# A refitted build-time timing model and a new order of work in a one-core attention and feed-forward kernel

## The chip, the core and the metric

The kernel runs on one core of a Trainium2 chip. A core has a matrix engine (TensorE, shown as PE, with its weight loads as PEld), a vector engine (VectorE, DVE), an activation engine (ScalarE, ACT), a general engine (GpSimd, POOL) and a queue engine that only issues transfers (SyncE, SP). Each engine runs its own instruction list in order, and the lists meet through semaphores. The metric is the device time of one execution in microseconds (us).

## The reference

The input `x` has 2048 rows of 640 values. After a layer norm it goes through two branches, which are added to the input:

```python
xn  = layernorm(x)
q   = (xn @ wq) -> 32 heads of width 20;  k = xn @ wk;  v = xn @ wv   # one k and one v for all heads
p   = softmax(q k^T * 20 ** -0.5)          # 32 heads x 2048 x 2048
A   = (p v, heads side by side) @ wo
B   = silu(xn @ w1) @ w2                   # 640 -> 1728 -> 640
out = x + A + B
```

The scores are the large object: 32 x 2048 x 2048 values pass through an exponential.

## The kernel before

**Tiling of the attention.** The queries are cut into four chunks of 512, the keys into 16 tiles of 128. One *block* is the score tile of one head, one query chunk and one key tile: 128 keys by 512 queries, which is one PSUM bank. There are 32 x 4 x 16 = 2048 blocks. Four heads make a group, and consecutive blocks go round the four heads. The head width is 20, padded to 32, so a score matmul uses 32 of the 128 rows of TensorE and four blocks of four different heads run side by side (L1182, called S below). A fifth block of the same run has to wait for the row strip of the first.

**Exponentials.** A block takes one of two ways. On ScalarE one `Exp` activation reads one to four adjacent banks and writes bf16 (L1217). On VectorE one instruction turns the scores into 16-bit integers whose bits, read as bf16, approximate the exponential (L1234); three such blocks make a set, and for a set two shifted copies are made: one on VectorE or GpSimd, the other always on GpSimd (L1262 and L1268). A ScalarE block needs one matmul with the values `v`, a VectorE block three. Four of these matmuls, one per head, make one step called P (L1079), which adds into bank 7, kept for it. The other seven banks serve the score blocks and the third kind of matmul.

**Other work.** Projections, the feed-forward branch and the output projection run as steps called J (L541), four matmuls of 32 columns side by side, 512 or 320 wide. The feed-forward branch also needs 54 `Tanh` activations (L1456).

**What sets the order.** The instruction lists are made at build time by a planner. It keeps a clock for each engine, and gives every operation a modelled duration and a time at which its result is seen by others (`LAT`). For ScalarE, VectorE and GpSimd it takes the next ready operation by priority. TensorE follows from block 70 on a written string, `ORDER`, one letter for each action (`follow`, L860). `P` and `J` are the steps named above. Any other letter is a *visit*: it issues the S matmuls of the next 1 to 4 blocks, and `VISITS` says how many blocks and how many of them go to VectorE. Upper case puts the first shifted copy of a set on VectorE, lower case on GpSimd. A visit waits until the planner's model has enough banks free (`s_banks`, L706) and until the exponentials' buffer of 26 slots has room (`room`, L931); if it has none, P steps are put in ahead of it. In `do_S` (L1143) the planner chooses the banks, orders the S matmuls by the modelled time at which each bank comes free, and forms one `Exp` for each run of adjacent banks. S matmuls planned for the same moment share one semaphore increment, that of the last of them (`seal`, L1139).

The planner's times are not in the program. The program has only the order on each engine, the choice of banks, the cut into `Exp` instructions, the side of each shifted copy, and the waits that follow.

Of the kernel before, what the change touches and what calls it, by code (L numbers as in the profile page):

```python
# [22 lines left out]
S = 2048  # L23
# [42 lines left out]
SWITCH = 0.106  # L66
FIRST = 0.01
T_PE = 0.2155
S_AGAIN = 0.09
REL = {"act": 0.07, "dve": 0.04}  # L70
LATE = 0.2
T_S = 0.2085
S_GAP = 0.0035
S_LEAD = 0.9
PV_PRESS = 12
DVE_TH = 0.6
# [9 lines left out]
ORDER = (
    "KmkmmkPhKFPgkPPPKMmgMPPCKPgPfPPgMPKhPCKPPmGPHJkBJJPBJbPPJJGmJJJJmkmPKKKPPMkkPMkmBJPkKMPJPJhkPJKkmJPH"
    "KPMKPFkPPMkkPJPMKhPPbJJGkJcMKJkPgHHBhPPghKmPemJPPJJJJPGhKJJPMJBJmgJmgPJJJJJPPPPBPBPBPJGMPJbMGPPbPPGJ"
    "PKkhPPPJPFJPKmPPkGMPPJJJBJJbPPfPPkKmPPJJPJKkMPJPJPfPJJJJJJJMAJPJJJJmkKMkJJPJBKPPPPBPPMGKJJJJPJMGmkPJ"
    "PPPJPPPfJPPJPPJMMgKJJJJJMgKJPJJJKmbPJCPPaPJJkmPJmMkkJJPgGPJJPJJhkmJJJPJJmaJJJJJPgmPBMPPPBPPMGMPPGMJP"  # L90
    "JBJJJPJJMGkkMJJPJPgmJJPgmPJPJkkmPfPPPBPPMaPJPPJPBJJJPBPmgPJPJbJJPJbJPJPmgJJJJJGmJJBPPFMKKPPbMPPPaJJG"
    "mJJPJPbJJJJMkKPJJJGMPJJMKKPPfbPMkkPPmgMAPPJPJPJgMJJPBPMKKJJJJPJPmGPJPJbJJJPgMJJJJKMKPEfPPPbPPFPPBJPP"
    "PJgmPPJJPGMJJaPJJBJJJJJJEPPPPfPPPMgPFPPJJGMJBJJMGJPPJbPJJPJJJPPPPKGJPPJJJPJJFPPJGPPMBPPmGPPPKGmPPPFP"
    "PBPJPJPJBMGJJPJPPgmJJgMJJPGMJJJJGmPfPgmePJJJBPJJgmPJJMGJJPJmMAkPPPPPHkPJJPMgMJJJPmKHkJJJJPJmKGJPJJJk"
    "HPcPJmHgJJJJJKBbmPPGmPPKhPJJJJJBbPPPJJPJPbJgMJPbPJJJJJBJJJJJgmbPPPPPgmmPPbPJPbJJJJbgmPPPPPGMmPPPBPPJ"
    "JJBJJbbJJJJJbGMMkKPPkmgPPPJPJPPbMJJPJPGbJJJJJbPPmKkmPPPgMPJJMGJPJJPEHPPPPBJJJJBJPJkKmJJJJgMJJJJJmkKJ"
    "JJJhKFfbhHPPgMPAPPPJJPgMJJJPaMPbPPPPfPJPgJPMKMKJPJPPJPPJGmJJmgJJJgmJJJJJMgJJPBPJAPfPPPPMMGPmmGgJJJJP"
    "JJBJmGPJJPJPbJJPGmmGJJJPPJBPPJJbJPmgPPFPPbPPJKgJJJJbmbPPBJPJGMPJJMgJJJmGJJPMgJPJgMJPPmGPBPJJmGJPJJGm"
    "JJbPPPkmGPPgMJPJJJJgKMJJJPJJPMKgMJJJJKMKPPJgmJJPJbPJmgmhKPPKkMPEPPPPfPPmgPBJJmgJJJbPfPPgmPJJJJPMkkBJ"
    "JJJJJJJEJPJJJKhJPJJPBPPmkKkPPPPPMCGPPPmKKPJPJmGPPPPJGMPPJJJgmPJPPJbJJJJbJJbPJJbPJhKPmgPJJmgPFPPMGMmG"  # L100
    "PPJJGJJPJPPPJPgMkJJPJPkKPJJGmmJPJPJBJBJJPJJBPPEPPPPfPPbPPbPPfPPbPJJJJJbGMPPPJJPJgmPBJJJJJMAmJJPEPJPJ"
    "PJkmJJePJJJJJPbBPPPPPbmPhKPJJGmJJPJMGKPPPPPbBPPJJPJGMmJJPJJPhGmJJJJJJFJJPEJJPJJJPgMmGPPPPMgJPJPBJPJb"
    "JPBPPPmKkMPkHPJJJBJbPJJJbPJJJGMPJJJhKJmGPJPGmPPFPPBJJJJJgkMkmPPPJJPfJJJGmgmAPPbPPJPJbmJPPbJGMPJgmJPJ"
    "BPPJMgJJJmGJPgmJPJJJamJPPPJcGJPJJMKkJPJJgMPPbmPPkgPPJPBMJJPGJJJFPJJJJgmJJJbJPJgMPbJJJJPmABJJPJPeJJPP"
    "bbMPPmgPPPBmPBmgPPPhHPJGJPPJKMgJJJJJBJJmgJPJJkkmJJJJKmkJPJBmPPKHMAPPJPPJPJJBJPHkJPkMkJPJJJmkgJJJJPbJ"
    "PJKmKJPJJHBPPPMaPPPPcKPPbPPmkkPPKmkMJJPJBJJgMPHkJPmGPPJPJPfJPPPPJJHkmkPJJPJJJmKKkJJJJJPmkkJPPJJfBPBP"
    "FPPgmPPGMJJJMGJJJbJPJPmgPJJmGJPgMJJPBJPPbJJBPJJGmBJPPbPPEJJJPJMgJPPJJJPkBPJJJJJJkmGJJPPMbPJPJmgMgJPP"
    "bPPMbPPKmkPPEPJPJJJJMGPJJBJJJJmgPBJJJBJJJJmgJmgPPfPPBPPgmKPPHkPJPPJJhJPJJGhPJJJPJePPPPMgPPFPPBJJJbJJ"
    "bJJPJPcJJPePJJJJJKmKHKPPPPPPPgkMHPPPPmBJJPJKkMJPJJPmbKJPJJJMAPJJJJJGkmmJJJJJPPgmGmPPPPPkhMJJJJJemKPP"
    "PPPKHmJJJbmPJJPggMJPJPPPgMJJkmPJmAPJJJHJJPmGBPPPPPPbPPJJJPJmGJJJJGmJPJmGJJBPJJmgJJPJbJPJmGPfPgmPPPBP"  # L110
    "PHGPJJJJJJGKMJPPJJJkmBJJJJBJJJJJBFPPAPPPfPPPPFPPGmJJJJMgJJJHkPPPJaJJJPJPPKMkJPJPJJJJJCkPambPPPPmkMKP"
    "kkMfPbPPPPJPJgmJPbJPJPJBBJPPJbPBJPPJgMPJJBPJJJMgJJJJmGPAMPJPPJJJJPbJJJBJPJBPJJBmgJJJJkmkJJJPMkaMGMPP"
    "PPMaPPPPFPPGmPPPPFPBPJPJbJJbPPJGMJPJJPmgJbPPJJPJJMAJJPJJBPJJgmPPBMPPBPPPMAPPGmPPJJJPJJEJJJJJJgMPJBJJ"
    "JJbJJJfPbPBPPmMgePmGPJPJJJEPPJPJPJBJPJJJmGPPJPJBJPJPPJbPPJBJbPPJgmPPFbPBFPPbPMbGMbPPmGMgBPPPGPPPaPMG"
    "PPPPPmPgmPPeMgMPbMPePmGPPPPPBPPMaBJJJJJJBJPJBPEPPAP"
)
Z_COST = 0.2
U_PRIO = 1.022
# [40 lines left out]

class Op:  # L160
    __slots__ = ("eng", "dur", "fn", "deps", "prio", "seq", "end", "avail", "idx", "inc", "inc_no", "sem",
                 "on_sched", "name", "dma", "mode", "start", "mm", "work", "then", "lock", "rep", "tile", "kt", "w", "x", "na", "at")

    def __init__(self, eng, dur, fn, deps, prio=0.0, name="", on_sched=None, mode=None):
        self.eng = eng
# [28 lines left out]
class Sched:  # L194
    def __init__(self, nc, stack):
        self.nc = nc
        self.stack = stack
        self.engs = ("pe", "act", "dve", "pool", "sp")
        self.order = {e: [] for e in self.engs}
        self.t = {e: 0.0 for e in self.engs}  # L200
        self.pend = {e: [] for e in self.engs}
        self.lastw = {}
        self.readers = defaultdict(list)
        self.seq = 0
        self.nsem = 0
# [48 lines left out]
    def ready(self, op, extra=0.0):  # L254
        r = op.at
        for d in op.deps:
            if d.avail is None:
                return INF
            if d.eng == op.eng and not d.dma:
                if op.eng == "pe" or op.eng == "sp":  # L260
                    a = d.end
                else:
                    a = d.avail - OWN[op.eng]
            else:
                a = d.avail
# [12 lines left out]

    def commit(self, op, start):
        e = op.eng  # L280
        op.start = start
        op.end = start + op.dur
        if op.dma:
            if op.name in ("oTd", "xTd", "uTd"):
                self.dma_t = op.end
            self.dma_t = max(getattr(self, "dma_t", 0.0), op.end) + op.mode / (270e3 if op.end < 13.5 else RATE)
            op.avail = op.end + T_LAND.get(op.name, 1.6) if op.name in ("oTd", "xTd", "uTd") else max(op.end + 2.0, self.dma_t + 1.6)
        else:
            op.avail = op.end + LAT[e]
# [160 lines left out]
class Builder:  # L450
# [692 lines left out]
    def do_S(self, n, now, nd=None):  # L1143
# [919 lines left out]
```

## Time and profile before

| | |
|---|---|
| median of three runs | 680.37 us (lowest 678.98) |
| the profiled execution, its own time | 680.39 us |
| its span, first to last instruction | 678.6 us |
| PE busy | 670.4 us (99%) |
| ACT busy | 662.1 us (98%) |
| DVE busy | 615.3 us (91%) |
| POOL busy | 566.2 us (83%) |
| granted TensorE clock | 0.997 |

The profiled execution took 1.8 us more than its span. "Busy" is the time in which at least one instruction of the engine is in flight. Instructions of one engine overlap, so a busy share close to 100% doesn't say by itself that the engine could take no more: what counts is the distance from one instruction to the next.

### The profile page before, as it was taken

What the parts mean: (1) busy time and instruction counts of PE and PEld (TensorE: products, weight loads), DVE (VectorE), ACT (ScalarE), POOL (GpSimd) and SP (SyncE); (2) the same over time, 40 slices, a digit from 0 to 9 for tenths busy, and PEclk for the clock granted to TensorE, in tenths of its full rate; (3) what the DMA queues carried; (4) which work ended last, traced back from release to release, by engine and by line L of the source; (5) the groups of instructions that cost most, each with busy time, mean ns of one, the idle gap of its engine ahead of it and who ended that gap; (6) DMA issues with size and microseconds to landing.
All of it is one profiled execution on the core that took longest, in us unless ns stands there. A gap on an engine that the chain in (4) does not pass through costs nothing.

```text
span 678.6 us, 22121 instructions
## 1 busy us (share of the span) xinstructions
PE 670.4 (99%) x9663; PEld 239.9 (35%) x9663; DVE 615.3 (91%) x1093; ACT 662.1 (98%) x852; POOL 566.2 (83%) x466
## 2 busy tenths in 40 slices
PE   9999999999999999999999999999999999999998
PEld 4433233333333333333333333333333333333324
DVE  8799989998999999999899899899989998998996
ACT  6899999999999999999999999999999999999996
POOL 6588898888878988886989987988898999878873
PEclk9899999999999999999999999999999999999999
DMA  7358300001003000101102000011012100000003
GB/s 207 79 196 269 80 18 15 7 15 15 18 17 57 10 10 17 36 15 32 29 19 60 10 18 21 27 17 33 14 29 47 31 2 20 10 19 19 20 17 64
DMA packets 51895, 27.81 MB, mean 41 GB/s; under 512 B 37750, under 2 KB 51158, under 8 KB 51798
## 3 DMA queue, kind: packets, MB, share of 16 engines
q1 hardware_dynamic: 51510, 26.07, 15.2%
q8 instruction: 75, 1.23, 0.8%
q10 hardware_dynamic: 288, 0.33, 0.1%
q14 instruction: 22, 0.18, 0.1%
HBM read 11.44 MB, written 2.62 MB: 21 GB/s over the span
## 4 chain that ended last, share of the span: by engine, by line
PE 50%; ACT 49%; issue 0%; DVE 0%; ACTq 0%
ACT sbt L1217 47%; PE psall L1079 17%; PE psall L1182 16%; PE psall L541 15%; ACT sbt L1456 2%; PE psall L999 1%; PE psall L1954 1%; PE psall L1446 0%; PE psall L1358 0%; PE psall L1935 0%; PE psall L1378 0%; ACT sbt L1803 0%; ACT sbt L1559 0%; PE psall L1498 0%; PE psall L1332 0%
## 5 line engine op out<-in xcount | busy, mean ns | idle before, releaser
L1217 ACT ACTIVATE sbt<-psall 128x1024 bf16<-128x1024 f32 (+2 forms) x773 | 632.1, 1001 | 3.6 <-PE psall L1182 3.2
L1268 POOL TENSOR_TENSOR sbt<-sbt 128x768 int32<-128x768 int32 (+2 forms) x376 | 525.0, 1424 | 84.2 <-DVE sbt L1262 78.4
L1234 DVE TENSOR_SCALAR sbt<-psall 128x512 int16<-128x512 f32 x708 | 461.2, 684 | 45.8 <-PE psall L1182 39.4
L1079 PE MATMUL psall<-sbt 128*32 128x512 bf16 x3464 | 284.2, 383 | 0.0
L1182 PE MATMUL psall<-sbt 32*128 32x512 bf16 x2048 | 258.1, 385 | 2.6 <-ACT sbt L1217 1.8
L541 PE MATMUL psall<-sbt 128*32 128x320 bf16 (+1 forms) x3863 | 239.0, 331 | 0.0
L1182 PEld LDWEIGHTS psall<-sbt 32*128 32x128 bf16 x2048 | 70.1, 91 | 226.5 <-ACT sbt L1217 124.8
L541 PEld LDWEIGHTS psall<-sbt 128*32 128x32 bf16 x3863 | 89.4, 95 | 88.5 <-issue 44.9
L1079 PEld LDWEIGHTS psall<-sbt 128*32 128x32 bf16 x3464 | 75.3, 95 | 103.2 <-issue 69.3
L1262 DVE TENSOR_SCALAR sbt<-sbt 128x1536 int16<-128x1536 int16 (+2 forms) x112 | 60.3, 552 | 0.3
L1464 DVE SCALAR_TENSOR_TENSOR sbt<-sbt,psall 128x512 bf16<-128x512 bf16 (+1 forms) x56 | 37.9, 678 | 0.2 <-ACT sbt L1456 0.2
L1456 ACT ACTIVATE sbt<-psall 128x512 bf16<-128x512 f32 x54 | 36.0, 666 | 0.0
L1300 POOL TENSOR_TENSOR sbt<-sbt 128x320 bf16<-128x320 bf16 x31 | 22.6, 729 | 5.6 <-DVE sbt L1262 4.8
L1312 DVE CAST sbt<-psall 128x512 bf16<-128x512 f32 x31 | 21.1, 682 | 0.6 <-PE psall L1079 0.4
L999 PE MATMUL psall<-sbt 128*128 128x512 bf16 (+6 forms) x56 | 15.5, 416 | 1.9 <-DVE sbt L1717 1.2
L1562 DVE SCALAR_TENSOR_TENSOR sbt<-psall,sbt 128x320 bf16<-128x320 f32 x28 | 13.3, 486 | 1.7 <-PE psall L541 1.4
L1413 DVE TENSOR_SCALAR sbt<-psall 128x512 bf16<-128x512 f32 (+1 forms) x19 | 13.0, 683 | 0.8 <-PE psall L541 0.4
L1783 DVE BATCH_NORM_STATS2 sbt<-sbt 128x6 f32<-128x320 bf16 x26 | 11.3, 465 | 2.4 <-DMA sbt<-in_A_x_dram 2.4
L1809 POOL TENSOR_SCALAR sbt<-sbt 128x640 bf16<-128x640 bf16 x8 | 7.0, 874 | 6.4 <-DVE sbt L1813 3.4
L999 PEld LDWEIGHTS psall<-sbt 128*128 128x128 bf16 x56 | 5.4, 108 | 8.9 <-issue 3.8
L1295 DVE RECIPROCAL sbt<-sbt 128x16 f32<-128x16 bf16 x31 | 7.5, 244 | 0.0
L1954 PE MATMUL psall<-sbt 128*128 128x256 bf16 x40 | 6.8, 310 | 0.6 <-ACT sbt L1217 0.6
(87 smaller groups left out, 81.0 us busy)
## 6 DMA issues: line engine op xcount, KB each, us to landing
sbt<-in_A_x_dram SPq DMA_DIRECT2D x31, 160.0 KB, 3.5
out_dram<-sbt SPq DMA_DIRECT2D x15, 160.0 KB, 1.8
sbt<-in_B_w_dram SPq DMA_DIRECT2D x5, 432.0 KB, 5.1
sbt<-sbt SPq DMA_DIRECT2D x105, 20.0 KB
sbt<-in_B_w_dram SPq DMA_DIRECT2D x13, 160.0 KB, 2.8
sbt<-sbt SPq DMA_DIRECT2D x1, 1024.0 KB, 7.3
sbt<-sbt SPq DMA_TRANSPOSE x56, 2.4
sbt<-in_A_wo_dram SPq DMA_DIRECT2D x5, 160.0 KB, 2.9
```

The source lines that it names most:

```text
L541: ins = pe.matmul(self.bk(b, 0, n, j, j + SLOT), w[:, j:j + SLOT], x, start=start, stop=stop, tile_position=(0, j), skip_group_check=True)
L999: return pe.matmul(self.bk(b, 0, n), self.zero[:, 0:P], self.zero[:, 0:n], start=True, stop=True)
L1079: ins = pe.matmul(self.bk(UBANK, 0, QW, r, r + SLOT), self.v[:, it.w, it.kt, :], it.x(), start=f, stop=False, tile_position=(0, r), skip_g ...
L1182: return pe.matmul(self.bk(bank[i]), self.kT[r:r + SLOT, 1 if i in dv else 0, kt * P:(kt + 1) * P], self.qT[r:r + SLOT, g % 8, (g // 8) % ...
L1217: return a.activation(self.E[:, (b0 + lo) * QW:(b0 + lo + m) * QW], self.ps[:, b * BANK:(b + m) * BANK], AF.Exp, scale=ACT_SCALE)
L1234: return v.tensor_scalar(self.Z[:, zs, zp * QW:(zp + 1) * QW], self.bk(bb), 0.0, ZMAX, ALU.max, ALU.min)
L1262: sc.new("dve", td, lambda v, k=k: v.tensor_scalar(self.Y[:, zs, k, 0:w], self.Z[:, zs, 0:w], float(PH[k + 1][0]), None, ALU.add), zk, yk, ...
L1268: sc.new("pool", tp, lambda v, k=k, cb=cb: v.tensor_tensor(self.Y[:, zs, k, 0:w].bitcast(I32), self.Z[:, zs, 0:w].bitcast(I32), cb, ALU.ad ...
L1300: op = sc.new(eng, 0.75 if eng == "pool" else t_dve_ps(16 * DH), lambda v: v.tensor_tensor(dst, ut[:, :, :, 0:DH], rb, ALU.mult), [key, (" ...
L1312: ev = sc.new("dve", t_dve_ps(QW), lambda v: v.tensor_copy(self.U[:, up, :], self.bk(UBANK)), [("UB",)], [("U", up)], prio=U_PRIO, name=f" ...
L1456: sc.new("act", t_act(QW), lambda a: a.activation(t, src, AF.Tanh, scale=0.5), [("B", b)], [("tb", tp)], prio=X_PRIO, name=f"th{c}_{fk}")
L1464: sc.new("dve", t_dve_ps(QW), lambda v, r0=r0, r1=r1, ht=ht: v.scalar_tensor_tensor(out=ht[r0:r1, :], in0=t[r0:r1, :], scalar=1.0, in1=src ...
```

## The change

The model's constants and rules are changed, and the string is another one. No operation is added to the kernel's mathematics.

In the model: a visit's S matmul is charged 0.092 instead of 0.106 us for entering its mode, the step after a visit up to 0.1315 us, an activation's completion can run behind its issue (each activation completes no sooner than its duration plus 0.0125 us after the one before it), a bank is counted free from that completion, some pairs of engines get their own latency, and S matmuls planned within 0.037 us of each other share an increment, with their increments 0.037 us apart.

In the string the actions are, counted from the two versions:

| | before | after |
|---|---|---|
| P letters / J letters | 860 / 936 | 862 / 934 |
| visits | 1055 | 701 |
| visits of 1 / 2 / 3 / 4 blocks | 502 / 252 / 232 / 69 | 75 / 112 / 377 / 137 |
| blocks in all, on VectorE, on ScalarE | 1978, 694, 1284 | 1978, 698, 1280 |
| visits with 0 / 1 / 2 / 3 / 4 ScalarE blocks | 321 / 237 / 444 / 53 / 0 | 62 / 69 / 500 / 69 / 1 |
| unbroken runs of visits (no P or J between) | 531 | 527 |
| further rounds of four blocks in these runs | 91 | 90 |
| sets whose first copy is on GpSimd / VectorE | 116 / 115 | 109 / 123 |

The first 70 blocks are issued before the string begins, in both. Two new forms of visit are there, `i` (four blocks, all on ScalarE, used once) and `l` (two blocks, both on VectorE, used 12 times). The diff, with the two strings cut to their first and last lines:

```diff
-REL = {"act": 0.07, "dve": 0.04}
+REL = {"act": 0.075, "dve": 0.045}
...
+S_IN = 0.092
+P_IN = 0.1315
+INC = 0.037
+ACT_MORE = 0.0125
+PAIR = {("act", "dve"): 0.17, ("dve", "pool"): 0.163}
...
-VISITS = {"a": (3, 0), "b": (3, 1), "c": (3, 2), "e": (4, 1), "f": (4, 2), "g": (2, 0), "h": (2, 1), "k": (1, 0), "m": (1, 1), "d": (4, 3)}
+VISITS = {"a": (3, 0), "b": (3, 1), "c": (3, 2), "e": (4, 1), "f": (4, 2), "g": (2, 0), "h": (2, 1), "k": (1, 0), "m": (1, 1), "d": (4, 3), "i": (4, 0), "l": (2, 2)}
 ORDER = (
-    "KmkmmkPhKFPgkPPPKMmgMPPCKPgPfPPgMPKhPCKPPmGPHJkBJJPBJbPPJJGmJJJJmkmPKKKPPMkkPMkmBJPkKMPJPJhkPJKkmJPH"
...
-    "PPPPPmPgmPPeMgMPbMPePmGPPPPPBPPMaBJJJJJJBJPJBPEPPAP"
+    "hkCblgbfACBPPAcPPPBPBfJJJMgcPJJhPggPPJFJPJJJbgmMPPPHPPJAPJPPPCPJPeJPFJkPGPEcPPBFPPJbPaJCJJJEBLAJBJPB"
...
+    "BJJBJJJPbPBPPJJbJBJPBPJFJPPmGBPFbPPPBePPBPPPfPPbPfAPPFPPbhPPMEKPmkPPBPPPfPPMgPPePPJJJGJPPFPGJJPIP"
 )
...
+                if self.fine and not d.dma and (d.eng, op.eng) in PAIR:
+                    a += PAIR[d.eng, op.eng] - LAT[d.eng]
...
-            op.avail = op.end + LAT[e]
+            op.cmp = op.end
+            if e == "act":
+                op.cmp = self.act_done = max(op.end, self.act_done + op.dur + ACT_MORE) if self.fine else op.end
+            op.avail = op.cmp + LAT[e]
...
-                    r = max(r, d.end + REL[d.eng])
+                    r = max(r, d.cmp + REL[d.eng])
...
+        if self.pe_mode == "S" and mode != "S" and 0 <= self.at:
+            return max(P_IN - SWITCH, P_IN - idle)
...
-        dur = T_S + SWITCH if timed else T_PE + 0.004 * (n > 3) + self.switch("S")
+        dur = T_S + S_IN if timed else T_PE + 0.004 * (n > 3) + self.switch("S")
...
-            if timed and due[i] > at + 1e-9:
+            if timed and due[i] > at:
+                if due[i] > at + INC:
+                    self.seal(group)
+                    group = []
                 at = due[i]
-                self.seal(group)
-                group = []
...
+        if timed:
+            heads = [sop[i] for i in turn if sop[i].rep is None]
+            for a, c in zip(heads, heads[1:]):
+                if c.avail < a.avail + INC:
+                    for q in sop:
+                        if q is c or q.rep is c:
+                            q.avail = a.avail + INC
```

More of the change, by code (lines that the diff above doesn't have):

```diff
@@ L84 @@
 YIELD = 0.65
-VISITS = {"a": (3, 0), "b": (3, 1), "c": (3, 2), "e": (4, 1), "f": (4, 2), "g": (2, 0), "h": (2, 1), "k": (1, 0), "m": (1, 1), "d": (4, 3)}
+VISITS = {"a": (3, 0), "b": (3, 1), "c": (3, 2), "e": (4, 1), "f": (4, 2), "g": (2, 0), "h": (2, 1), "k": (1, 0), "m": (1, 1), "d": (4, 3), "i": (4, 0), "l": (2, 2)}
 ORDER = (
-    "KmkmmkPhKFPgkPPPKMmgMPPCKPgPfPPgMPKhPCKPPmGPHJkBJJPBJbPPJJGmJJJJmkmPKKKPPMkkPMkmBJPkKMPJPJhkPJKkmJPH"
[L88 to L114, printed above, removed]
-    "PPPPPmPgmPPeMgMPbMPePmGPPPPPBPPMaBJJJJJJBJPJBPEPPAP"
@@ new lines @@
+    "hkCblgbfACBPPAcPPPBPBfJJJMgcPJJhPggPPJFJPJJJbgmMPPPHPPJAPJPPPCPJPeJPFJkPGPEcPPBFPPJbPaJCJJJEBLAJBJPB"
+    "PJJbPmgJhJPGmBPBPJJPBPPJPPPbPJPEPPBPJJJJJBblGPBPPPBPPkbPJPJPfPJJPJPGBJJJJJBfPPBPPJPPbPPPJPHkJJJPfJJJ"
+    "JJPEJJJJJJBhJJJJPhGPPPBPPFJJJJJBgPJPPJJFJJPPBHJJJJPJJePJJPJfJPPPKePPJJHPJJePJPPKfJPJPPPBJJJPJPbJJJJJ"
+    "PmgbPJPJJPGlPbPPPfPPBJJJJBJPPJJBBPPJPPJPPBJJJbPJJbPPfBPPPePJPJJBPPJJPPPMGJPPPJPbPJJbJgMPJJBPJJPJJJbJ"
+    "JPBPPGLPbPPPBPEPPPJJJbPJPGPFJJJPJBPJPbJPJbJJJPmGPHgPPPPfJPJJPbJBJPBJbPJJJPbJJJJbPJJPBJbPJJJPePPPFPPP"
@@ new lines @@
+    "BPFPPJJBJJPBJJJaPJJPJbJJJJBPePPPPfPPPPfPAPJJJbJJPbJJJJbJJJPBPJbJJJPBJJJbfPPBEPPPPFPPbPJPJaJKLJPJPJBP"
+    "BJJJJbJJJbJfPhkePPJJPJbJJbPJPMGJJJJBBPPPPPBPJJJmbJJPPbhPJJJJJPehPPJJJFPPJJbhJPJJJJePPPPPBPFPPBJPJbJP"
+    "GmJPJBPPPJJJJJbPPJJbJJJBJJJJJPHePPPPPBPMbPJPJCJJJbPPbPPPFPPMgJPJJBJJBBJJPBJPJJMgPPPgMPPkbPJPJPJPPlGJ"
+    "JPPBgJJJJJbPPFPPBPJPBJJJJePPPPPkMbJJJPbJJJJJBJJbJJJJJhkJJJJbFbfBPBPPEPPJPJbJPJJAPPfPPPPfPPJgPJPFJJJP"
+    "JbJJGMJPJJJJfGJJPJJJJbfPPBFEPJPJJKFJJPPbJPMkKJJPJJPgbPPJJJJJJPJfJJPgPPbPFPPPBPPEPJJPbPJbJJPFPBPPbPJJ"
@@ new lines @@
+    "BJJJJJBJPPBJPJbJJBJJJGmJPJBJPJPmGePJJJJbPPPJPPJPJEJPJPJJCGJPPBPJJbJPJBJPPbJJPbPFPPPPhgPPPFPPJJbJPbJb"
+    "JPPbPPFPPbJJJJbJbJJJJJJEJJPJJbJJJJbPPePPPPPhFPPPBPPBJPJJbJJJbJJPBJJBJJJbPJBJPBJPBPPJJJBPmgMPKgfPJPJJ"
+    "JJJbJPJBJJPbJJJbFJJgJPPJePJPPJbPBMPPPBPPGlPPbJPJbJJJbBPPPPPJPJPbPJPPbJPPPJBJJJJJbPBPJPPPJJJJPbbPPJJJ"
+    "JJMGBPPPPPfPPBJJCJJJPEPPPPBPPPPkGJJJPBmJJPPJmhgJJPJJCkPJJJJJeJJJJPJPBmgPPPPBPJPJbPPPJPJbJPPbPbPPFPPJ"
+    "PPJBPJJJfgPPPJJBJJJbJJJPBJJBfPJJbJJJPFGPBJJJJJfgPhKPPPeJPJJbJHkJPPPFPBPJPJbPJJBJJJBPJJBPJPBJPJBPbJJJ"
@@ new lines @@
+    "JBJPJJBPPGlPPaPPPPbbPPJPJJJMbJJJJGJJJGmmJJPJJbJJJJbPghBPPJJJJPePPPPPJPPPBbPfPBPPFPPPbPPEPPPJPJPJBPJJ"
+    "JJbPJBJJJJJBJbJJJJJbfPPBPEPPJPJPJJbJPJPJBPbJJJJBJJJBBPJBJJJJbfPPBPEPPPPFPPbPJPJJBbPJJPPfPPbPBJJJJbPJ"
+    "JJJPPJJbbPJJJJJbJJJbJfPPbFPBPPJPBJJbJPJPamPPJJJEPPJFPJJJJBJPbJJPbJJbPJPBPPPEPPJJPJPBJPJJBJJPJBJJPBJJ"
+    "JBPJbJJPbPJJPGmPfPPPBPPbPPeJJJPJBJJPbJJJPBJPBJJJJBJPJJbJPJBPfBPPePJPJBPJPPJJPePJJPJhJJEPPPPbPPPBmPPb"
+    "PJJBPJmgJcJJJJJJJeJPPJJJlGGbPPhhPJJPBJPbJPJPPJkhHPJJJPJPalJJJJJHgJPJPPBJcJPJPeJJJJJPbBPPPPPFPPBJPPGm"
@@ new lines @@
+    "JJJJPbKMkPPPJJJFPJJPEJJJJJPGMbPPPPbPJJJPJPPPBPPPJJJJBJJBJJJPBPJbJJJbJPJBfPPPBPPMbPJJgJJJJEJJPJPgMJJJ"
+    "bJJPJBJJJJmGPPGLPBEPPmgCKJJJJJJbJPPbPPJPbPPPPJJJJJJeJPJJJPPJgEPPPPfPPPPbmPPPbPPfPPPbJPJJJBPcPPbJJPBJ"
+    "BJJJPJBPbJJJJJBJJBJEPPJJJJGmJJJBPPJJPJPbJJbPJPJBBJPPbJJbJJPBPPbMPbPPEPBPPPPPPfPPbPJPbJPPJBJPJBJPPbJJ"
+    "PJPJPePPJPPJPJJBPJJJJJBPmgPPfPPBPPfPJJPAJPBJJJJJJJeJJPPJJbJJJbJJBPfPBPPFPPPePbPPPPJPEJJPJPJJPgJPJfJP"
+    "BJJBJJJPbPBPPJJbJBJPBPJFPPmGBPFPbPPPBePPBPPPfPPbPfAPPFPPbhPPMEKPmkPPBPPPfPPMgPPePPJJJGJPPFPGJJPIP"
@@ L161 @@
     __slots__ = ("eng", "dur", "fn", "deps", "prio", "seq", "end", "avail", "idx", "inc", "inc_no", "sem",
-                 "on_sched", "name", "dma", "mode", "start", "mm", "work", "then", "lock", "rep", "tile", "kt", "w", "x", "na", "at")
+                 "on_sched", "name", "dma", "mode", "start", "mm", "work", "then", "lock", "rep", "cmp", "tile", "kt", "w", "x", "na", "at")
     def __init__(self, eng, dur, fn, deps, prio=0.0, name="", on_sched=None, mode=None):
@@ L210, in __init__ @@
         self.last_add = None
+        self.act_done = 0.0
+        self.fine = False
     def sem(self, name):
@@ L766, in step @@
             self.at = 0
+            sc.fine = True
         if 0 <= self.at < len(ORDER):
```

## The prediction

> **What bounds the kernel now.** The page's busy shares come first, then the chain of work that ended last, then stretches of the run.
>
> ```profile
> PE 670.4 (99%) x9663; PEld 239.9 (35%) x9663; DVE 615.3 (91%) x1093; ACT 662.1 (98%) x852; POOL 566.2 (83%) x466
> ...
> PE 50%; ACT 49%; issue 0%; DVE 0%; ACTq 0%
> ```
>
> ```profile
> 200.00:300.00 100.00, 99.79 (x1474) 34.64 (x1474) 93.42 (x160) 99.61 (x131) 87.42 (x67) 1.00 0.11 24
> 500.00:600.00 100.00, 99.87 (x1519) 35.58 (x1516) 90.99 (x155) 100.00 (x133) 88.45 (x66) 1.00 0.09 21
> ```
>
> In the second fence the columns after the length are busy time (and count) of PE, PEld, DVE, ACT and POOL, then the granted clock, the DMA share and GB/s. PE and ACT are both busy all the time and the chain is shared evenly, so these views can't say which of the two is full. The distance from one instruction to the next can. ScalarE first, in order of time:
>
> ```profile
> 234.18 0.64 ACT L1456 ACTIVATE sbt<-psall 128x512 bf16<-128x512 f32 x1
> 234.66 1.08 ACT L1217 ACTIVATE sbt<-psall 128x1024 bf16<-128x1024 f32 x1
> 235.56 0.67 ACT L1456 ACTIVATE sbt<-psall 128x512 bf16<-128x512 f32 x1
> 236.04 1.10 ACT L1217 ACTIVATE sbt<-psall 128x1024 bf16<-128x1024 f32 x1
> 236.96 0.68 ACT L1456 ACTIVATE sbt<-psall 128x512 bf16<-128x512 f32 x1
> ```
>
> Start plus duration gives the ends: 234.82, 235.74, 236.23, 237.14, 237.64. From end to end a one-bank activation takes 0.49 and 0.50 us, a two-bank one 0.92 and 0.91, while the starts are 0.48 and 0.90 to 0.92 apart and the durations creep up (0.64, 0.67, 0.68 for the same form). So the next instruction is always there before the last one ends, and completions are what is full. I take 0.49 us for one bank, 0.915 for two, hence 0.425 for each further bank (1.34 for three, 1.765 for four) and 0.065 fixed for each instruction. Now all of ScalarE's work by form, its first and last `Exp`, and its idle time:
>
> ```profile
> L1217 ACT ACTIVATE sbt<-psall 128x1024 bf16<-128x1024 f32 x467 | 458.0, 1111 | 0.9 <-PE psall L1182 0.7
> L1217 ACT ACTIVATE sbt<-psall 128x512 bf16<-128x512 f32 x256 | 147.4, 698 | 0.4 <-PE psall L1182 0.4
> L1217 ACT ACTIVATE sbt<-psall 128x1536 bf16<-128x1536 f32 x50 | 75.1, 1518 | 2.3 <-PE psall L1182 2.2
> L1456 ACT ACTIVATE sbt<-psall 128x512 bf16<-128x512 f32 x54 | 36.0, 666 | 0.0
> ```
>
> ```profile
> 15.03 2.79 ACT L1217 ACTIVATE sbt<-psall 128x1536 bf16<-128x1536 f32 x2 [0.24 <-PE psall L1182]
> 17.71 0.92 ACT L1803 ACTIVATE sbt<-sbt 128x640 bf16<-128x640 bf16 x1
> ...
> 23.26 0.92 ACT L1803 ACTIVATE sbt<-sbt 128x640 bf16<-128x640 bf16 x1
> 26.10 7.86 ACT L1217 ACTIVATE sbt<-psall 128x1536 bf16<-128x1536 f32 x7 [1.92 <-PE psall L1182]
> 34.26 14.04 ACT L1217 ACTIVATE sbt<-psall 128x1024 bf16<-128x1024 f32 x18 [0.30 <-PE psall L1182]
> ```
>
> ```profile
> 638.98 31.17 ACT L1217 ACTIVATE sbt<-psall 128x1024 bf16<-128x1024 f32 x31
> ```
>
> 467 x 0.915 + 256 x 0.49 + 50 x 1.34 + 54 x 0.49 = 427.3 + 125.4 + 67.0 + 26.5 = 646.2 us of completions. They lie between 15.03 and 638.98 + 31.17 = 670.15, 655.1 us. Of the 8.9 us left over, the waits shown at 26.10 and 34.26 take 2.2 and the two activations at 17.71 and 23.26 less than 1.9. Some 5 us are left in which ScalarE could have worked and didn't, in 635 us. ScalarE is full.
>
> TensorE, the same way, by rows in order of time: a stretch of wide J steps, two rounds that begin with S, and a stretch of narrow J steps:
>
> ```profile
> 299.79 1.05 PE L541 MATMUL psall<-sbt 128*32 128x512 bf16 x16
> ...
> 301.64 0.39 PE L1182 MATMUL psall<-sbt 32*128 32x512 bf16 x3
> ...
> 301.96 0.62 PE L1079 MATMUL psall<-sbt 128*32 128x512 bf16 x8
> ...
> 302.51 0.39 PE L1182 MATMUL psall<-sbt 32*128 32x512 bf16 x3
> ...
> 302.83 0.32 PE L541 MATMUL psall<-sbt 128*32 128x320 bf16 x4
> ...
> 304.68 0.59 PE L541 MATMUL psall<-sbt 128*32 128x320 bf16 x12
> ```
>
> Two P steps take 0.62 us with the 0.39 of the last in it, about 0.22 a step (four J steps of 512: (1.05 - 0.39) / 3 = 0.22), a step of 320 (0.59 - 0.32) / 2 = 0.135. From S to the next step it is 301.96 - 301.64 = 0.32, and back 302.51 - 301.96 = 0.55 for two steps, 0.11 more than these need. A run of visits so costs 0.43 us whatever is in it, up to four blocks, and about 0.22 more for each further round of four.
>
> ```profile
> L1079 PE MATMUL psall<-sbt 128*32 128x512 bf16 x3464 | 284.2, 383 | 0.0
> L541 PE MATMUL psall<-sbt 128*32 128x320 bf16 x2448 | 133.0, 302 | 0.0
> L541 PE MATMUL psall<-sbt 128*32 128x512 bf16 x1415 | 106.0, 382 | 0.0
> ```
>
> ```profile
> PEld psall L1182 <- ACT sbt L1217: 124.8, 347, 0.7
> ...
> PEld psall L1182 <- issue: 40.3, 120, 0.4
> DVE sbt L1234 <- PE psall L1182: 39.4, 117, 1.1
> PEld psall L1182 <- DVE sbt L1234: 38.9, 107, 0.4
> ```
>
> In fours: 866 P and 354 wide J steps at 0.22, 612 narrow ones at 0.135, 531 runs at 0.43 and 91 further rounds at 0.22: 268.4 + 82.6 + 228.3 + 20.0 = 599 us, in the same 635 us. That leaves at most 36 us. From below: an S weight load behind nothing but the switch stands 40.3 / 120 = 0.336 us, behind ScalarE 124.8 / 347 = 0.360, behind VectorE 38.9 / 107 = 0.364, so the waits for banks come to 347 x 0.024 + 107 x 0.028 = 11 us. TensorE has 11 to 36 us to spare, and ScalarE about 5.
>
> **The change part by part.** *ScalarE's instructions.* Visits with one block there go from 237 to 69, with two from 444 to 500, with three from 53 to 69, with four from none to one: 734 instructions become 639, and 1284 blocks 1280. At the distances above that is -168 x 0.49 + 56 x 0.915 + 16 x 1.34 + 1.765 = -82.3 + 51.2 + 21.4 + 1.8 = **-7.9 us** (95 instructions at 0.065 and four blocks at 0.425). The profile has 773 `Exp`s; the 39 above 734 belong to the first 70 blocks and to visits whose banks weren't adjacent. I keep 39. Were no visit split the gain would be at most 39 x 0.065 = 2.5 us larger; three times as many splits cost 5.1.
>
> The Trainium skill has another price: ScalarE: Activation LUTs, What ACT_TABLE_LOAD costs, puts the overlap of back-to-back activations at about 93 ns, out of 186 ns beyond the elements, which leaves about 93 ns fixed for each instruction. By that (an estimate from the page) the same edit would bring 95 x 0.093 + 1.7 = 10.5 us. The ends above give 65 ns, and the sum goes by them.
>
> *TensorE.* Four runs fewer (-1.7), two P steps more (+0.4), one further round less (-0.2), two J steps that move from the string to the tail (nothing): -1.5 us. Merging visits inside a run spares nothing, since the 0.43 us is paid for each run. Its need falls to about 597 us, in 635 - 7.9 = 627. Its room shrinks to 5 to 30 us, so ScalarE still decides.
>
> *Shared increments.* An `Exp` can now wait up to 0.037 us (the diff's own window) for the last S matmul of its visit. ScalarE's queue hides that: it sat idle for PE only 0.7 + 0.4 + 2.2 = 3.3 us in all, and mostly before 34.3. Without that cover 639 x 0.037 = 24 us would be the extreme; from below it is nothing, or a little less waiting, since fewer increments are sent. I take nothing.
>
> *VectorE and GpSimd.*
>
> ```profile
> L1268 POOL TENSOR_TENSOR sbt<-sbt 128x768 int32<-128x768 int32 x351 | 505.5, 1466 | 79.0 <-DVE sbt L1262 73.2 <-DVE sbt L1234 5.4
> L1234 DVE TENSOR_SCALAR sbt<-psall 128x512 int16<-128x512 f32 x708 | 461.2, 684 | 45.8 <-PE psall L1182 39.4
> L1262 DVE TENSOR_SCALAR sbt<-sbt 128x1536 int16<-128x1536 int16 x103 | 56.9, 565 | 0.2
> ```
>
> Four blocks and eight copies more on VectorE: 4 x 0.684 + 8 x 0.565 = +7.3 us at most, against 678.6 - 615.3 = 63 us idle. Six copies fewer on GpSimd (2 x 116 + 115 = 347 to 2 x 109 + 123 = 341): -8.8 us, against 112 us idle. Both are hidden. If VectorE's cover went, its 7.3 us would nearly undo the gain. The same transfers are issued, and the DMA share of 0.09 to 0.11 leaves their queues free.
>
> *The model's constants* are worth only the order they make. What they may do is change the 5 us of ScalarE's starvation. Visits that need two or three adjacent banks at once, with less spare on TensorE, should starve it somewhat more; a model that has completions running behind issue, as the ends above show them, should starve it less. Bounds: -5 (none left) and, from the slow rival below, +12. I take **+1.9**, near the lower end, because rows show the present starvation that low in spite of 237 one-block visits and an order that follows the older model.
>
> Sum: 680.39 (the profiled execution, 0.02 above the median) - 7.9 + 1.9 = **674.4 us**, a span of about 672.6.
>
> **The rivals.** *TensorE is the bound.* For it: 99% busy, and half of the chain. Against it: the 11 to 36 us above. Then only its own 1.5 us goes: 678.9 us. The Trainium skill speaks for it: TensorEngine Tiling (Array Packing), Key Properties, says that a change of tiling mode drains the engine, and 527 runs against 531 change modes as often. The 0.32 us from S to the next step agree that the drain is paid, not that it is what ends last.
>
> *ScalarE starves: slower.* Seven banks serve ScalarE, VectorE and the J step in hand. A one-block visit can use any bank that comes free; a visit of two or three ScalarE blocks needs neighbours. If one in seven of the 570 `Exp`s with two or more blocks finds its pair late by one P step of 0.22, 81 x 0.22 = 18 us are lost and the time is 680.4 - 7.9 + 18 = 690.5; one in ten gives 685. It decides against the change from 36 such waits on (7.9 / 0.22). For it: VectorE already stands 39.4 us waiting for S. Against: the runs keep their number and size, so banks are asked for nearly as often as now.
>
> *The merge doesn't happen.* If a visit's banks aren't adjacent the `Exp` is cut up again. At one in five of 570 it is 114 x 0.065 = 7.4 us, and the time about 680. Against it: at most 39 extra instructions now, among 497 visits of two or more.
>
> **How the numbers follow.** The forecast, ScalarE bound with 669 to 677.5 us, has 0.55; TensorE as the bound (677.5 to 681) 0.18; the merge lost (679 to 682) 0.05; ScalarE starved (681 to 695 and above) 0.19; better than 669, starvation and splits both gone, 0.03. The range of 668.5 to 686 leaves out the far part of starvation and little else. Faster by over 2% means below 666.8, which would take more than 7.9 + 2.5 + 3 us; slower by over 2% means above 694.0. Two per cent is about what a measurement of this kernel can tell from no change. So 0.02, 0.93 and 0.05.
>
> **What would show it.** Right: about 678 `Exp`s (`Exp` is the only L1217 instruction now; its line will move), some 70 to 80 of one bank and over 510 of two; end-to-end distances as before; ScalarE's sum about 638 us, with 5 to 8 us not used until its last `Exp` ends near 664; waits of S weight loads on ScalarE still near 0.36 us each. TensorE as the bound: S waits near 0.336 each, and ScalarE with bare gaps. Starvation: idle before `Exp` of 15 us or more, or ends more than 1 us apart for two-bank forms. A merge lost: more than 750 `Exp`s. The prediction fails most easily if the order found by the new model keeps banks later than the model thinks.

## The result and the profile after

The changed kernel takes 674.75 us (median of six runs, 673.87 to 676.02), the kernel before 679.34 in the same runs: a ratio of 0.9933 with a 95% interval of 0.9916 to 0.995, or 4.6 us less. One of the six executions of the kernel before was a slow one of 853.69 us, which the ratio leaves out; without it their median is 678.98. The profiled execution took 676.02 us with a span of 674.2, against 680.39 and 678.6, which is 4.4 us less. The forecast was 674.4 us, 6.0 less than the profiled execution of the kernel before.

The busy shares of the changed kernel and the head of its chain of work that ended last:

```profile
PE 666.6 (99%) x9666; PEld 240.2 (36%) x9669; DVE 622.6 (92%) x1109; ACT 656.6 (97%) x766; POOL 552.0 (82%) x454
...
PE 82%; ACT 15%; DVE 2%; issue 0%; ACTq 0%
```

The busy shares say as little as before. The chain says more: it was shared 50 to 49, and now runs through PE for 82%. ScalarE's groups by form (busy time, mean ns of one, idle time before them), then its first and its last `Exp`s in order of time:

```profile
L1236 ACT ACTIVATE sbt<-psall 128x1024 bf16<-128x1024 f32 x530 | 504.2, 1058 | 1.8 <-PE psall L1193 1.1
...
L1236 ACT ACTIVATE sbt<-psall 128x1536 bf16<-128x1536 f32 x58 | 85.4, 1483 | 2.4 <-PE psall L1193 2.3
...
L1236 ACT ACTIVATE sbt<-psall 128x512 bf16<-128x512 f32 x98 | 56.8, 630 | 0.0
...
L1475 ACT ACTIVATE sbt<-psall 128x512 bf16<-128x512 f32 x54 | 33.8, 625 | 0.2 <-PE psall L549 0.2
...
L1236 ACT ACTIVATE sbt<-psall 128x2048 bf16<-128x2048 f32 x1 | 2.0, 1983 | 0.0
```

```profile
15.45 2.79 ACT L1236 ACTIVATE sbt<-psall 128x1536 bf16<-128x1536 f32 x2 [0.41 <-PE psall L1193]
```

```profile
628.53 37.14 ACT L1236 ACTIVATE sbt<-psall 128x1536 bf16<-128x1536 f32 x38
```

The distances from end to end are as before; four activations in order of time:

```profile
233.37 1.04 ACT L1236 ACTIVATE sbt<-psall 128x1024 bf16<-128x1024 f32 x1
234.29 0.60 ACT L1475 ACTIVATE sbt<-psall 128x512 bf16<-128x512 f32 x1
234.76 1.04 ACT L1236 ACTIVATE sbt<-psall 128x1024 bf16<-128x1024 f32 x1
235.67 0.63 ACT L1475 ACTIVATE sbt<-psall 128x512 bf16<-128x512 f32 x1
```

They end at 234.41, 234.89, 235.80 and 236.30, so a one-bank activation takes 0.48 and 0.50 us and a two-bank one 0.91. There are 687 `Exp`s where there were 773. By the distances of the prediction, ScalarE's sum is 530 x 0.915 + 98 x 0.49 + 58 x 1.34 + 1.765 + 54 x 0.49 = 638.9 us, 7.3 less than the 646.2 before. The stretch from the first `Exp` to the end of the last is 665.67 - 15.45 = 650.2 us, 4.9 less than 655.1. So what ScalarE didn't use rose from 8.9 to 11.3 us. The mean of a two-bank `Exp` fell from 1111 to 1058 ns: it overlaps less with the one before it, which fits a ScalarE that is less pressed.

### The profile page after: what moved, and what is told of

It is laid out like the page before. It is cut to its first block, busy times and chain, and to the rows that moved or that the text cites. A ratio compares the mean times of both kernels' runs of the same rounds, so it can differ in the third digit from the quotient of the medians.

```text
span 674.2 us, 22041 instructions
## 1 busy us (share of the span) xinstructions
PE 666.6 (99%) x9666; PEld 240.2 (36%) x9669; DVE 622.6 (92%) x1109; ACT 656.6 (97%) x766; POOL 552.0 (82%) x454
## 4 chain that ended last, share of the span: by engine, by line
PE 82%; ACT 15%; DVE 2%; issue 0%; ACTq 0%
PE psall L1090 28%; PE psall L1193 26%; PE psall L549 25%; ACT sbt L1236 15%; DVE sbt L1253 2%; PE psall L1010 2%; PE psall L1973 1%; PE psall L1465 0%; DVE sbt L1281 0%; PE psall L1954 0%; PE psall L1397 0%; DVE sbt L1331 0%; PE psall L1377 0%; ACT sbt L1822 0%; DVE sbt L1483 0%
## 5 line engine op out<-in xcount | busy, mean ns | idle before, releaser
L1236 ACT ACTIVATE sbt<-psall 128x1024 bf16<-128x1024 f32 (+2 forms) x687 | 624.1, 1034 | 4.2 <-PE psall L1193 3.4
L1287 POOL TENSOR_TENSOR sbt<-sbt 128x768 int32<-128x768 int32 (+2 forms) x364 | 511.0, 1429 | 94.9 <-DVE sbt L1281 88.2
L1193 PEld LDWEIGHTS psall<-sbt 32*128 32x128 bf16 x2048 | 69.2, 91 | 219.2 <-ACT sbt L1236 126.7
L549 PEld LDWEIGHTS psall<-sbt 128*32 128x32 bf16 x3863 | 89.2, 95 | 90.4 <-issue 48.2
L1090 PEld LDWEIGHTS psall<-sbt 128*32 128x32 bf16 x3472 | 77.2, 95 | 103.7 <-issue 69.4
L1281 DVE TENSOR_SCALAR sbt<-sbt 128x1536 int16<-128x1536 int16 (+2 forms) x124 | 68.5, 566 | 0.4
L1475 ACT ACTIVATE sbt<-psall 128x512 bf16<-128x512 f32 x54 | 33.8, 625 | 0.2 <-PE psall L549 0.2
L1010 PE MATMUL psall<-sbt 128*128 128x512 bf16 (+5 forms) x51 | 14.8, 435 | 2.0 <-DVE sbt L1736 1.2
L1802 DVE BATCH_NORM_STATS2 sbt<-sbt 128x6 f32<-128x320 bf16 x26 | 11.3, 466 | 2.5 <-DMA sbt<-in_A_x_dram 2.5
```

Source lines behind the costliest of these rows:

```text
L549: ins = pe.matmul(self.bk(b, 0, n, j, j + SLOT), w[:, j:j + SLOT], x, start=start, stop=stop, tile_position=(0, j), skip_group_check=True)
L1010: return pe.matmul(self.bk(b, 0, n), self.zero[:, 0:P], self.zero[:, 0:n], start=True, stop=True)
L1090: ins = pe.matmul(self.bk(UBANK, 0, QW, r, r + SLOT), self.v[:, it.w, it.kt, :], it.x(), start=f, stop=False, tile_position=(0, r), skip_g ...
L1193: return pe.matmul(self.bk(bank[i]), self.kT[r:r + SLOT, 1 if i in dv else 0, kt * P:(kt + 1) * P], self.qT[r:r + SLOT, g % 8, (g // 8) % ...
L1236: return a.activation(self.E[:, (b0 + lo) * QW:(b0 + lo + m) * QW], self.ps[:, b * BANK:(b + m) * BANK], AF.Exp, scale=ACT_SCALE)
L1281: sc.new("dve", td, lambda v, k=k: v.tensor_scalar(self.Y[:, zs, k, 0:w], self.Z[:, zs, 0:w], float(PH[k + 1][0]), None, ALU.add), zk, yk, ...
```

## The experiments

The question was which engine the gain was taken from, where it stopped, and whether the model or the string brings it. My theory at first: ScalarE is the bound, each instruction of it costs about 0.065 us, and TensorE has room.

**The refitted model with the old string, and the old model with the new string.**

```diff
 # e1: the changed kernel
-VISITS, ORDER of the changed kernel
+VISITS, ORDER of the kernel before
 # e2: the kernel before
-VISITS, ORDER of the kernel before
+VISITS, ORDER of the changed kernel
```

> The refitted model with the old string. The plan it makes has 801 Exp instructions (34 of three banks, 471 of two, 296 of one) where the kernel before has 773 (50, 467, 256). ScalarE bound (my theory): +40 x 0.49 + 4 x 0.915 - 16 x 1.34 = +1.8 us on the 679.3 of before, 680 to 682. If the better fit of the model is what brings the gain: 675 to 677. If TensorE is the bound: 679, nothing moves.

> The old model with the new string (and its two visit forms). The plan has 699 Exp instructions (one of four banks, 51 of three, 532 of two, 115 of one). ScalarE bound: -141 x 0.49 + 65 x 0.915 + 1.34 + 1.77 = -6.5 us, with up to 2 us of new starvation: 673 to 675. If the fit of the model brings the gain: 678 to 680. If TensorE is the bound: 678.

Measured: the first 690.59 us (ratio 1.0156, 1.0135 to 1.0178), the second 685.33 (1.0075, 1.0055 to 1.0095). Both are misses for every theory that I had written down, and both are slower than either kernel. The clock alone doesn't explain that: the one execution of each at a mean clock of 1.0 took 688.88 and 682.63 us. The second has ScalarE's work nearly down to that of the changed kernel, and yet takes 10 us more. The next row is its two-bank `Exp`s:

```profile
L1213 ACT ACTIVATE sbt<-psall 128x1024 bf16<-128x1024 f32 x532 | 508.9, 1062 | 7.4 <-PE psall L1178 6.6
```

The idle time for PE is 7.4 us, where the same group of the changed kernel has 1.8. A string and a model are a pair: once they were parted, counting instructions missed the time by some 9 to 12 us in both runs.

**The merged instructions taken apart again.** Two doses, in the changed kernel; no order, bank or wait differs. The edit, shortened:

```diff
+if m == 2 and b_at >= 70 and self.n2 % 6 == 0:     # e4: % 2
+    a.activation(E, first bank, AF.Exp, scale=ACT_SCALE)
+    return a.activation(E, second bank, AF.Exp, scale=ACT_SCALE)
 return a.activation(E, both banks, AF.Exp, scale=ACT_SCALE)
```

> The changed kernel, with every sixth two-bank Exp after block 70 issued as two one-bank Exps over the same banks, one wait before and one increment after the pair; order, banks and all else as they are. 85 or 86 instructions more, which is what the change removed. ScalarE bound: 86 x 0.065 = +5.6 us, 678.5 to 680.5. If the order is what brings the gain, or if TensorE is the bound: less than 1 us, 675.

> As the run before it, with every second two-bank Exp in two: 257 instructions more. ScalarE bound: 257 x 0.065 = 16.7 us, 689 to 692. TensorE the bound, with some 6 us of slack on ScalarE: 685 at most.

Measured: 678.82 us (ratio 0.9982, 0.9971 to 0.9993) and 688.47 (1.0121, 1.0104 to 1.0138). Against 674.75 that is +4.1 for 85 instructions and +13.7 for 257. The first lies in the range that I gave for ScalarE as the bound, the second 0.5 us below it. The first gives back most of the gain, nearly all by the medians and some three quarters by the two ratios (0.9933 and 0.9982), and neither the order nor TensorE's work was touched, so the saved instructions carry it. From the first dose to the second it is (688.47 - 678.82) / 172 = 0.056 us an instruction, somewhat under the 0.065 that I took from the ends. The Trainium skill, ScalarE: Activation LUTs, What ACT_TABLE_LOAD costs, has figures that leave about 93 ns for each further activation (an estimate from the page). No run here shows that much, and the measurement decides.

**More work for TensorE.** Into both kernels go steps of zeros, which change no sum (the edit shortened):

```diff
+if self.npv > 30 and self.npv % 13 == 0 and len(items) == 4 and not any(first):
+    for r in range(0, P, SLOT):
+        pe.matmul(the P step's 32 rows of bank 7, self.zero[:, 0:SLOT], self.zero[:, 0:QW], start=False, ...)
```

> The changed kernel with 60 steps more on TensorE: after every thirteenth P step four matmuls of zeros into the same sums, 60 x 0.216 = 12.9 us of work, nothing else moved. ScalarE bound with 5 to 30 us of room on TensorE (my theory): +2 to +8 us, 677 to 683. TensorE the bound: the whole 12.9, 687 to 688.

> The kernel before with 59 steps of zeros more on TensorE (12.7 us of work), put in as in the changed kernel. My theory now, some 5 us of room on TensorE: 685 to 688, +6 to +8. With 11 us of room or more, as I predicted it: 679 to 683. TensorE the bound already: 691 to 692.

Measured: the changed kernel 684.87 us (1.0071, 1.0054 to 1.0089), the kernel before 687.18 (1.0108, 1.0091 to 1.0125). In the changed kernel 10.1 of the 12.9 us come through, so TensorE has about 3 us of room there and not 5 to 30; the run missed my range and stopped short of the rival's. (All four executions had a mean clock of 1.0; against those of the changed kernel at 1.0, near 674, it is 10.9 us, and the room 2.) In the kernel before 7.3 of 12.7 come through: about 5 us of room, as I expected by then.

**Less work for ScalarE.** In both kernels 64 two-bank `Exp`s do one bank only, and the probabilities of the other block are left as they stand in the buffer.

```diff
+if m == 2 and b_at >= 70 and self.n2 % 8 == 0:     # kernel before: % 7
+    return a.activation(E, first bank, AF.Exp, scale=ACT_SCALE)
 return a.activation(E, both banks, AF.Exp, scale=ACT_SCALE)
```

> The changed kernel with 64 two-bank Exps reading and writing one bank only (their second block is left out, so those probabilities are stale): 64 x 0.425 = 27.2 us less on ScalarE. ScalarE the bound, with TensorE next at 5 to 30 us below: 655 to 669. TensorE the bound already: 672 or more.

> The kernel before with 64 two-bank Exps reading and writing one bank only (their second block is left out): 27.2 us less on ScalarE. My theory now, ScalarE the bound before the change with TensorE some 5 us behind it: 672 to 676. As I predicted it, with 11 to 36 us of room on TensorE: 655 to 669. TensorE the bound already before: 678 or more.

Measured: the changed kernel 673.61 us (0.9907, 0.9886 to 0.9928), the kernel before 674.86 (0.9926, 0.991 to 0.9941). The first missed my range by 4.6 us and met the rival's, TensorE as the bound. By the second run I had changed my theory, and it met that. 27 us less on ScalarE bring 5 us before the change, and 1.1 us after it, which the two intervals can't tell from nothing. Both kernels stop near 674, and there the chain is TensorE's. First the page of the kernel before with less on ScalarE (the chain and the `Exp` group), then that of the changed one:

```profile
PE 91%; ACT 6%; DVE 2%; DMA 0%; issue 0%; POOL 0%; ACTq 0%
...
L1221 ACT ACTIVATE sbt<-psall 128x1024 bf16<-128x1024 f32 (+2 forms) x709 | 582.8, 933 | 11.3 <-PE psall L1182 7.3
```

```profile
PE 93%; DVE 3%; ACT 3%; DMA 0%; issue 0%; POOL 0%; ACTq 0%
...
L1240 ACT ACTIVATE sbt<-psall 128x1024 bf16<-128x1024 f32 (+2 forms) x623 | 574.1, 1009 | 18.1 <-PE psall L1193 14.2
```

The idle time shown is small beside the 27 us, since most gaps between activations are shorter than their overlap and count as busy. The chain is the better witness. It doesn't say that TensorE's own work is all that stands at 674. The weight loads of S in the changed kernel with less on ScalarE:

```profile
PEld psall L1193 <- ACT sbt L1240: 110.3, 310, 0.8
...
PEld psall L1193 <- issue: 52.9, 157, 0.4
```

They still stand 110.3 / 310 = 0.356 us behind ScalarE, against 52.9 / 157 = 0.337 behind nothing. How much of the 674 us is TensorE's list, and how much is waiting for banks to come back, these runs don't tell apart.

**Single terms of the model.** Three of the new terms were taken out one at a time, each time under the new string. The others (`S_IN`, `P_IN`, `REL`) were not tried alone.

```diff
-ACT_MORE = 0.0125
+ACT_MORE = 0.0                                     # e7
-PAIR = {("act", "dve"): 0.17, ("dve", "pool"): 0.163}
+PAIR = {}                                          # e8
-INC = 0.037
+INC = 0.0                                          # e11
```

> The changed kernel planned without the backlog of activations in the model (the extra 0.0125 us set to 0); all other new terms and the new string stay. The plan has 692 Exps (5 more, +1.0 us by form). If this term is what makes string and plan fit: the time goes towards the 685 of the old model, 681 to 686. If it isn't: 675 to 677.

> The changed kernel planned without the latencies by pair of engines (the two entries taken out); the rest stays. The plan has 705 Exps (18 more, +1.2 us by form). If these latencies are what makes string and plan fit: 681 to 686. If not: 675 to 677.

> The changed kernel planned with the window for shared increments at 0. The lists of TensorE, VectorE and GpSimd are in the same order; 690 Exps instead of 687 (+0.3 us by form), and some S matmuls send an increment of their own. Sharing costs and spares nothing (my theory): 674.5 to 675.5. If it spares TensorE time: 677 or more. If it holds Exps up: 673 or less.

Measured: 683.93 us without the backlog (1.0049, 1.0026 to 1.0073), 685.04 without the latencies by pair (1.007, 1.0051 to 1.0089), 674.17 without shared increments (0.9915, 0.99 to 0.993). The first two lie where the term was to matter. The last is 0.3 us under my range, but its interval overlaps that of the changed kernel (0.9916 to 0.995), so sharing increments is worth nothing that can be measured. Each of the other two takes away the whole gain and more, for 5 and 18 `Exp`s. A good part is lost in one place. The next rows are the end of the run without the backlog, and then the same seven microseconds of the changed kernel, which is some 4 us further on in its work by then; the columns are those of the prediction's table by stretch, with the granted clock after the five engines:

```profile
655.00:662.00 7.00, 6.01 (x50) 1.18 (x48) 6.11 (x10) 5.73 (x7) 6.04 (x5) 0.71 0.08 19
662.00:668.00 6.00, 6.00 (x60) 1.75 (x57) 4.25 (x8) 4.45 (x5) 2.07 (x3) 0.77 0.53 37
```

```profile
655.00:662.00 7.00, 6.75 (x84) 2.12 (x83) 6.84 (x13) 7.00 (x9) 4.57 (x5) 1.00 0.34 77
```

From 655 to 662 us the first has TensorE issuing 50 matmuls instead of 84, ScalarE idle for 1.27 us, and a clock of 0.71. ScalarE's next pieces in the run without the backlog, with the wait before each:

```profile
659.64 2.43 ACT L1236 ACTIVATE sbt<-psall 128x1536 bf16<-128x1536 f32 x3 [1.27 <-PE psall L1193]
662.65 1.02 ACT L1236 ACTIVATE sbt<-psall 128x1024 bf16<-128x1024 f32 x1 [0.58 <-PE psall L1193]
664.60 3.36 ACT L1236 ACTIVATE sbt<-psall 128x1024 bf16<-128x1024 f32 x3 [0.92 <-PE psall L1193]
670.07 4.73 ACT L1236 ACTIVATE sbt<-psall 128x1024 bf16<-128x1024 f32 x4 [2.11 <-PE psall L1193]
```

That is 4.9 us of ScalarE waiting for S in the last 20 us before the tail. The run of the new string under the old model shows the same pieces there, 1.6 us later, the first three after waits of 1.28, 0.62 and 0.90 us:

```profile
661.26 2.43 ACT L1213 ACTIVATE sbt<-psall 128x1536 bf16<-128x1536 f32 x3 [1.28 <-PE psall L1178]
664.30 1.02 ACT L1213 ACTIVATE sbt<-psall 128x1024 bf16<-128x1024 f32 x1 [0.62 <-PE psall L1178]
666.23 3.34 ACT L1213 ACTIVATE sbt<-psall 128x1024 bf16<-128x1024 f32 x3 [0.90 <-PE psall L1178]
```

The run without the latencies by pair has them too:

```profile
661.11 2.43 ACT L1236 ACTIVATE sbt<-psall 128x1536 bf16<-128x1536 f32 x3 [2.22 <-PE psall L1193]
664.15 1.02 ACT L1236 ACTIVATE sbt<-psall 128x1024 bf16<-128x1024 f32 x1 [0.61 <-PE psall L1193]
```

Which bank or which operation of another engine stands wrong there was not traced, and neither was the rest of the loss. It also isn't shown that the refitted model finds better strings than the old one would: no other string was made here. What is shown is that this string needs the model that it came with, two of its terms one by one. Whether these terms matter because they are true of the chip, or only because the string was made to go with the plan that they give, isn't shown.

**More work in the prologue.** In some executions the clock is halved for 3.4 us near 23 us. The test put work just ahead of it.

```diff
+if n0 < 8 and k == DC - 1:
+    ins = pe.matmul(self.bk(b, 128, 512), self.zero[:, 0:P], self.zero[:, 0:384], start=True, stop=True)
```

> The changed kernel with eight matmuls of zeros (384 columns each) among the small matmuls for v near 19.5 and 22.3 us, into columns of the same bank that nobody reads; nothing else moved. If the executions with a mean clock of 0.997 lose their 2 us to the half-speed stretch near 23 us, and that follows from little work on TensorE just before it: all near 674, with a clock of 1.0. If the work of a few us doesn't decide it: 674 in some executions and 676 in others, as now.

Measured: 674.85 us (0.9929, 0.9917 to 0.9941). The first of the two expectations failed, and the second is near: of five executions one still had a mean clock of 0.997 and one 0.999, and the three at 1.0 took 674.57 to 674.85, against 673.87 to 674.01 of the changed kernel, so the filler itself seems to cost about 0.7 us. The place was also not the only one. In the traces of three other runs (the new string under the old model, the smaller dose of split `Exp`s, the changed kernel with less on ScalarE) the 3.4 us lie near 45 us, behind a stretch in which TensorE was busy. The last of them:

```profile
40.00:45.00 5.00, 4.90 (x64) 1.85 (x60) 4.93 (x9) 5.00 (x9) 4.60 (x4) 1.00 0.75 292
45.00:50.00 5.00, 4.75 (x49) 1.21 (x45) 4.00 (x8) 3.94 (x6) 5.00 (x4) 0.66 0.05 14
```

Whether the halving follows from little work stays open.

No experiment points to a version that clearly beats the changed kernel: by the less-work run about 1 us is left to gain on ScalarE alone, and more would have to come from TensorE's side.

## Why the prediction was right, and where a term was off

**The time: in part luck.** The forecast of 674.4 us is 0.35 off the median, but it started from an execution at a mean clock of 0.997, and the median lies between three executions at 1.0 and three at 0.997. Like with like, from profiled execution to profiled execution, 6.0 us were forecast and 4.4 came. They are -7.3 in ScalarE's sum, +2.4 in what it didn't use, and +0.5 ahead of its first `Exp` and behind its last.

**ScalarE as the bound before the change: right.** The kernel before gets 5 us faster when ScalarE is relieved, and TensorE's extra work comes through only for 7.3 of 12.7 us. The views that showed it were the distance from end to end and the sum over forms. The busy shares and the chain (99 to 98, 50 to 49) couldn't.

**-7.9 us by fewer instructions: right, a little large.** It was -7.3: 687 `Exp`s, not 678, because the first 70 blocks and the visits whose banks weren't adjacent added 48 and not the 39 that I kept. The merged instructions are the cause, as taking them apart again showed, so long as plan and string fit.

**+1.9 us of new starvation: right in size (+2.4) by luck, wrong in its reason.** I chose it between bounds of -5 and +12, and put it down to visits that need neighbouring banks. The runs point to TensorE instead, which nearly took over. With ScalarE relieved by 27 us, neither kernel gets far below 674 us, so no saving on ScalarE alone could have brought much more than 5.

**TensorE's room: the mis-sized term.** The prediction had 11 to 36 us before and 5 to 30 after, "so ScalarE still decides"; the runs show about 5 before, and 1 to 3 after, where both engines are close to deciding. The signs named for it are mixed: 11.3 us not used instead of 5 to 8, and S waits of 0.351 us behind ScalarE, between the 0.36 of one side and the 0.336 of the other. The sum from steps used 531 runs of visits and 866 P steps, as the string and the fours have them. The program's own TensorE lists have 588 and 589 runs of visits (the first 70 blocks and P steps put in between the visits of one run included) and 892 and 893 P steps, since some are not full. The P steps put in also cut long runs, so that only 57 and 53 further rounds of four are left of the 91 and 90. At the prediction's prices that is 57 x 0.43 + 26 x 0.22 - 34 x 0.22, some 23 us more, which leaves about 13 of the 36. The 23 us are the most that the counts can explain, since only 577 of the 588 runs lie in the 635 us that the sum was set against. The 13 us left are still 8 more than the runs show, and what takes these was not traced. The other estimate, 11 us from the mean waits of the S weight loads, was about as far off. The same means after:

```profile
PEld psall L1193 <- ACT sbt L1236: 126.7, 361, 0.6
...
PEld psall L1193 <- issue: 38.6, 115, 0.4
PEld psall L1193 <- DVE sbt L1253: 31.4, 87, 0.4
```

126.7 / 361 = 0.351, 38.6 / 115 = 0.336 and 31.4 / 87 = 0.361: 361 x 0.015 + 87 x 0.025 = 7.6 us, too high by some 5 as well. A mean difference of 0.02 us isn't all room: it was as large (0.356 against 0.337) with 27 us less on ScalarE.

**TensorE as the bound (0.18 of the chance): wrong for the time, right for the next step.** It gave 678.9 us, but TensorE stood near 674 and not near 679. With as many runs of visits as before (588 and 589) that place hardly moved: 674.86 us with ScalarE relieved before the change, 673.61 after, with intervals that overlap; the prediction gave TensorE 1.5 us less. The Trainium skill, TensorEngine Tiling (Array Packing), Key Properties, has every change of tiling mode drain the engine. No run here varies the number of changes, so the times don't test that.

**Starvation to 685 or 690, and the merge lost: not seen in the changed kernel.** VectorE's and GpSimd's cover held: VectorE's busy time rose by 7.3 us, as summed, to 622.6, GpSimd's fell. Times of that size did appear in the runs with string and model parted, 690.59 and 685.33 us, with a condition that I didn't name: a string and a plan that don't fit each other. Whether it was for want of neighbouring banks, as I had it, was not traced.

**Shared increments at nothing: right**, 674.17 us without them.

## What to carry to other kernels

Where two engines look full, sum each one's instructions by the distance between their ends, and take the counts from the program's own list and not from the script that it is made of: here that difference was up to 23 of the 36 us of room that I gave TensorE. How much room the second engine has, runs with known work added to it and taken from the first tell better than either sum. A saving on the fuller engine is worth no more than its lead over the next. An order written for one timing model belongs to that model: change one term of it alone and the order can lose more than the whole change brought, as two of three terms did here, so such parts are to be judged together.

## What the runs showed of the hardware that I had not expected

The mean clock of an execution (0.997 or 1.0) goes with its time. The changed kernel took 673.87 to 674.01 us in the three executions at 1.0, and 675.50 to 676.02 in the three at 0.997; the kernel before, beside the last experiments, 679.03 to 679.92 in five at 1.0 and 680.20 to 681.34 in four at 0.997. In the traces of both profiled executions the lower mean is one stretch of 3.4 us at half clock near 23 us. The changed kernel:

```profile
0.00:25.00 25.00, 22.13 (x174) 11.89 (x177) 20.09 (x75) 17.49 (x26) 15.63 (x50) 0.97 0.58 161
25.00:50.00 25.00, 24.55 (x261) 9.30 (x260) 20.08 (x37) 23.06 (x26) 18.07 (x18) 0.96 0.55 166
```

What the two rows miss of a full clock, 25 x 0.03 + 25 x 0.04 = 1.75 us, is about half of the 3.4. The run without the backlog term shows the same thing late. From 654 to 656 us TensorE was busy for 0.94 us:

```profile
654.00:656.00 2.00, 0.94 (x8) 0.20 (x6) 2.00 (x5) 2.00 (x3) 2.00 (x2) 1.00 0.00 0
```

By the rows of its end shown above 7 x 0.29 + 6 x 0.23 = 3.4 us of full clock are then missing, which is 6.8 us at half clock, just where the last exponentials have to be fed. Its four executions at 1.0 took 681.0 to 681.3 us, the six others 683.9 to 686.5. So most of what that run lost, some 7 of 9 us, it lost without the halved clock, and the halving goes with some 3 to 5 more. That the short lull brought it on is likely from the order of events, but not shown.
